# Reordering the start of a fused attention and MoE kernel: score bans ahead of their data, batch 2's scores ahead of batch 3's turn, MoE pieces moved in front of the first attention round

## The chip, the cores and the metric

The kernel runs on one core of a Trainium2 chip. The metric is device time in microseconds of one execution. Before the change it was 351.97 us, the median of three runs (351.76 to 352.08). PE is the matmul engine, DVE the vector engine, ACT the scalar engine, Pool the GpSimd engine; SP issues loads. A run is compared only with fast runs (executions that ran about as fast as the fastest of the same kernel).

## The reference

Eight batches of eight heads, 576 positions, head size 64. Forgetting attention (causal, with a decay from cumulated log gates), then a SiLU MoE layer with one expert over all 4608 tokens:

```python
scores = scale * q @ k.T + (cum[:, None] - cum[None, :])   # causal, log gates cumulated
attn   = softmax(scores); x = attn @ v                      # [4608, 512]
h = x @ w_in                                                # [4608, 2048]
out = (h * sigmoid(h)) @ w_out                              # [4608, 512], float32
```

## The kernel before

All engines' instruction orders are fixed by hand. The first 128 positions ("heads") of all batches are done first. For each batch: a *turn* (32 small matmuls, 16 for q and 16 for k, that transpose them, then copies out of PSUM by ACT and DVE), *scores* (8 matmuls, then an exp on ACT), *out* (8 matmuls with v, then a division on DVE), *back* (4 transposes of the result and a copy into x). Batches 0 to 3 form the first MoE group; when they are done the first MoE matmuls can start. Batches 4 to 7 are woven between MoE pieces, and then sixteen attention rounds for the other positions follow, R0 first, also woven with MoE pieces. A MoE piece is 4 matmuls: "m1" (x with w_in, tile `hp`) or "m2" (with w_out, tile `po`).

The causal mask is made in two ways. With a *ban*, two 128x512 matmuls put -30000 on the forbidden scores before the scores are added in PSUM, which costs PE time (0.53 us for two of them in the trace of before, 28.92 to 29.45 us). For batches 6 and 7 DVE multiplies the exponentials by a triangle after the exp instead (`mask0`).

```python
def ban0(b):                                   # needs no data of batch b
    sc = psc.tile([P, 2, NP, P], FP32, name="sc", tag="sc")      # psc: 2 buffers
    for i in range(2):
        nc.tensor.matmul(sc[:, i, :, :]..., lhsT=ident_bf, rhs=ban..., start=True, stop=False)
    return sc
# ... (cut)
def mask0(b):
    x = u0[b][:, :, :, :].rearrange("p i a t -> p (i a) t")
    nc.vector.tensor_tensor(out=x, in0=x, in1=tri[:, None, :].to_broadcast([P, H, P]), op=ALU.mult)
# ... (cut)
def convert_v(b, c):                           # weights v for an attention round, on Pool
    nc.gpsimd.tensor_tensor(out=vbf[b][r, c, :, :], in0=vst[b][c][r, :, :], in1=w_bf[...], op=ALU.mult)
# ... (cut)
keep_warm(1)                                   # one dummy 128x512 matmul
turn0(0, 1)
turn0(1, 0)
weights()
convert_v0(0); load_w_in(0)
scores0(0, ban0(0))
turn0(1, 1); turn0(2, 0); turn0(2, 1)
scores0(1, ban0(1))
convert_v0(1); load_v0(4)
out0(0, apart=True)
turn0(3, 0); turn0(3, 1)
scores0(2, ban0(2))
convert_v0(2); load_w_in(1); load_v0(5)
out0(1, apart=True)
back0(0, on_dve)
scores0(3, ban0(3))
convert_v0(3); load_qk0(4); load_w_in(2); load_qk0(5); load_w_in(3)
# ... (cut: out and back of batches 2 and 3, one more keep_warm(1))
load_qk(2); load_v(0, 2); load_v(0, 3); load_qk(3)      # loads for the rounds, on SP
for n in range(2):
    cast_qk(n); transposes(n)                            # Pool casts, SP transposes by DMA
# ... (cut: one more load)
for c in range(NM):
    convert_v(0, c)
fill(6.0)                                      # about 6 us of MoE pieces
two_more(4, True)                              # batches 4 and 5, banned
ready.add(1); fill(5.0); open2["w"] = True; fill(6.0, 2)
two_more(6, False)                             # batches 6 and 7, masked by DVE
```

The softmax here doesn't subtract the row's maximum and nothing guards it: scores larger than these inputs give would overflow.

## Time and profile before

| what | value |
|---|---|
| time | 351.97 us (351.76 to 352.08) |
| profiled execution | 351.23 us, span 349.5 us |
| PE busy | 340.0 us of 349.5 |
| first MoE matmul | 18.91 us |
| DMA share, every microsecond from 5 to 45 us | 1.16 or more (times of packets that overlap are added up, so it can pass 1) |

The head of the profile page: span and instruction count, then busy time of PE, and of part 2 (40 slices of the span, tenths) the granted PE clock and the DMA engines.

```profile
span 349.5 us, 9037 instructions
PE 340.0 (97%) x3645; PEld 204.3 (58%) x3645; DVE 188.8 (54%) x412; ACT 217.5 (62%) x400; POOL 123.6 (35%) x221
...
PEclk9999999999999999999999999999999999999999
DMA  8999999999996797596597589469620000010012
```

PE is busy nearly all the time (97%) at the full clock (mean 1.000), and DMA is full in the first eighth of the span (busy share 1.16 or more from 5 us on). So the only thing an order can win is PE's waits. The view of waits, for PE: engine, line, tile waited for, total us, times, longest (its first line, for the start-up dummies, is left out).

```profile
PE hp L544 <- ACT x L376: 0.8, 1, 0.8
PE tp L271 <- DMA qkb<-in_q_dram: 0.7, 1, 0.7
PE sc L445 <- ACT u L449: 0.5, 1, 0.5
PE tx L375 <- DVE xq L360: 0.5, 1, 0.5
PE dn L490 <- DVE gt L553: 0.4, 1, 0.4
PE dn L345 <- ACT u L312: 0.3, 1, 0.3
```

Where they stand, from PE's timeline: start, duration, operation, and in brackets the idle time before it and what ended it.

```profile
7.97 0.64 PE L271 MATMUL tp<-sel,qkb 128*64 128x64 bf16 x16 [0.75 <-DMA qkb<-in_q_dram]
18.91 1.46 PE L544 MATMUL hp<-x,w_in_bf 128*128 128x512 bf16 x6
38.83 5.40 PE L544 MATMUL hp<-x,w_in_bf 128*128 128x256 bf16 x48 [0.78 <-ACT x L376]
64.37 0.40 PE L445 MATMUL sc<-qkT 64*128 64x128 bf16 x8 [0.54 <-ACT u L449]
```

The first is batch 1's turn waiting for its q, the third the second MoE group waiting for ACT's copy, the last R0's scores waiting for an exp.

### The profile page before, as it was taken

Reading aid. Unit: us, or ns where it says so; the run is one execution under the profiler, and the core shown is the slowest. Engines: PE = TensorE matmul, PEld = TensorE weight load, DVE = VectorE, ACT = ScalarE, POOL = GpSimd, SP = SyncE. Lnnn points to the kernel's source line nnn. Section 1 sums busy time; section 2 is a strip of 40 time slices with the busy share of each in tenths; the row PEclk is TensorE's granted clock in tenths of the full one; section 3 lists DMA queues with packets and bytes.
Section 4 is the critical chain, followed back from the end, with each engine's and each line's share of the span. In section 5 each row is a group of like instructions: output and inputs, shape, how many; then the busy total and the mean of one; then the engine's idle time right before and its main releaser. Section 6 shows DMA issues by size and latency. Waiting matters only on the chain.

```text
span 349.5 us, 9037 instructions
## 1 busy us (share of the span) xinstructions
PE 340.0 (97%) x3645; PEld 204.3 (58%) x3645; DVE 188.8 (54%) x412; ACT 217.5 (62%) x400; POOL 123.6 (35%) x221
## 2 busy tenths in 40 slices
PE   7999999999999999999999999999999999999994
PEld 3645655566656656566565666656656565555663
DVE  4665925376666556466555664656745563534330
ACT  5766725886587675857768667595775934544431
POOL 7893156445282262273054225325320000010101
PEclk9999999999999999999999999999999999999999
DMA  8999999999996797596597589469620000010012
GB/s 159 226 205 201 198 199 196 240 184 189 196 205 152 155 148 172 124 199 152 125 206 145 125 189 147 114 160 188 130 54 34 32 32 30 30 63 30 32 60 60
DMA packets 136762, 47.92 MB, mean 137 GB/s; under 512 B 128017, under 2 KB 134417, under 8 KB 136721
## 3 DMA queue, kind: packets, MB, share of 16 engines
q1 hardware_dynamic: 127184, 31.75, 49.2%
q0 software_dynamic: 9376, 15.47, 18.7%
q8 instruction: 28, 0.46, 0.6%
q10 hardware_dynamic: 160, 0.13, 0.1%
q14 instruction: 14, 0.11, 0.1%
HBM read 36.85 MB, written 9.44 MB: 132 GB/s over the span
## 4 chain that ended last, share of the span: by engine, by line
PE 92%; ACT 3%; DMA 1%; issue 1%; DVE 1%; POOL 0%; POOLq 0%; ACTq 0%
PE po L589 36%; PE hp L544 35%; PE sc L445 7%; PE dn L490 5%; PE dn L499 3%; PE tp L271 2%; PE tx L520 2%; DMA qkb<-in_q_dram 1%; ACT u L449 1%; PE sc L286 1%; PE sc L305 1%; PE dn L345 1%; ACT osb L599 0%; PE tx L375 0%; ACT ut L461 0%
## 5 line engine op out<-in xcount | busy, mean ns | idle before, releaser
L552 ACT ACTIVATE th<-hp 128x384 bf16<-128x384 f32 (+2 forms) x208 | 95.4, 479 | 81.7 <-PE hp L544 79.9
L589 PE MATMUL po<-w_out_bf,gt 128*128 128x512 bf16 (+1 forms) x592 | 145.3, 374 | 0.0
L553 DVE SCALAR_TENSOR_TENSOR gt<-th,hp 128x384 bf16<-128x384 bf16 (+2 forms) x208 | 105.6, 522 | 70.6 <-ACT th L552 67.5
L544 PE MATMUL hp<-x,w_in_bf 128*128 128x384 bf16 (+2 forms) x704 | 128.8, 321 | 0.9 <-ACT x L376 0.8
L544 PEld LDWEIGHTS <-w_in_bf 128*128 128x128 bf16 x832 | 78.5, 98 | 53.9 <-issue 1.7
L449 ACT ACTIVATE u<-sc 128x1024 bf16<-128x1024 f32 (+1 forms) x96 | 74.9, 820 | 15.0 <-PE sc L445 15.0
L589 PEld LDWEIGHTS <-gt 128*128 128x128 bf16 x592 | 54.8, 98 | 49.8 <-issue 2.3
L568 POOL DMA_DIRECT2D out_dram<-osb x38 | 21.0, 553 | 174.0 <-ACT osb L599 138.5
L399 POOL TENSOR_TENSOR vp<-vf,w_bf 128x520 bf16<-128x520 f32 (+1 forms) x32 | 34.8, 1092 | 18.8 <-DMA vf<-in_v_dram 17.3
L454 DVE TENSOR_TENSOR u<-u,tri 128x768 bf16<-128x768 bf16 x32 | 23.1, 722 | 26.9 <-ACT u L449 26.9
L599 ACT ACTIVATE osb<-po 128x512 f32<-128x512 f32 (+1 forms) x37 | 22.0, 595 | 16.9 <-PE po L589 16.9
L445 PE MATMUL sc<-qkT 64*128 64x128 bf16 (+1 forms) x640 | 26.3, 207 | 0.5 <-ACT u L449 0.5
L445 PEld LDWEIGHTS <-qkT 64*128 64x128 bf16 x640 | 18.2, 94 | 9.9 <-issue 7.1
L461 ACT ACTIVATE ut<-sc 128x640 bf16<-128x640 f32 x32 | 23.1, 723 | 0.0
L468 DVE TENSOR_TENSOR ut<-ut,trit 128x128 bf16<-128x128 bf16 x32 | 7.8, 243 | 28.0 <-ACT ut L461 27.9
L490 PEld LDWEIGHTS <-u 128*128 128x128 bf16 x576 | 20.8, 97 | 3.4 <-issue 0.5
L490 PE MATMUL dn<-vp,u 128*128 128x65 bf16 x384 | 21.8, 193 | 0.0
L508 DVE TENSOR_TENSOR xr<-dn,rec 128x448 bf16<-128x448 f32 x32 | 20.0, 625 | 1.1
L490 PE MATMUL dn<-v,u 128*128 128x65 bf16 x192 | 19.8, 193 | 0.4 <-DVE gt L553 0.4
L385 POOL CAST qkb<-qf 128x384 bf16<-128x384 f32 x32 | 17.0, 532 | 4.1 <-DMA qf<-in_q_dram 3.6
L385 POOL CAST qkb<-kf 128x384 bf16<-128x384 f32 x32 | 17.2, 539 | 3.2 <-DMA kf<-in_k_dram 3.0
L544 PE MATMUL hp<-xt,w_in_bf 128*128 128x256 bf16 x128 | 17.7, 273 | 0.0
(67 smaller groups left out, 218.4 us busy)
## 6 DMA issues: line engine op xcount, KB each, us to landing
vf<-in_v_dram SPq DMA_DIRECT2D x32, 256.0 KB, 4.9
out_dram<-osb POOLq DMA_DIRECT2D x32, 256.0 KB, 2.7
qf<-in_q_dram SPq DMA_DIRECT2D x64, 96.0 KB, 3.0
kf<-in_k_dram SPq DMA_DIRECT2D x64, 96.0 KB, 3.0
w_in_bf<-in_moe_w_in_dram POOLq DMA_DIRECT2D x4, 512.0 KB, 8.7
w_out_bf<-in_moe_w_out_dram POOLq DMA_DIRECT2D x4, 512.0 KB, 12.9
qkb<-in_q_dram POOLq DMA_DIRECT2D x8, 128.0 KB, 6.0
qkb<-in_k_dram POOLq DMA_DIRECT2D x8, 128.0 KB, 6.2
```

Source lines behind the costliest of these rows:

```text
L385: nc.gpsimd.tensor_copy(out=t2[:, c0 : c0 + NR, :].rearrange("p c x -> p (c x)"), in_=t[:, :, :, :].rearrange("p c h d -> p (c h d)"),)
L399: nc.gpsimd.tensor_tensor(out=vbf[b][r, c, :, :], in0=vst[b][c][r, :, :], in1=w_bf[r, c + 1, b * H : (b + 1) * H, None].to_broadcast([n, H ...
L445: nc.tensor.matmul(sc[:, i, o : o + q1 - q0], lhsT=kt, rhs=t[r, q0:q1], start=True, stop=True)
L449: nc.scalar.activation(out=u[:, :, c * SM : c * SM + w], in_=sc[:, :, 0:w], func=ACT.Exp, scale=scale)
L454: nc.vector.tensor_tensor(out=x, in0=x, in1=tri[:, None, None, :].to_broadcast([P, 2, NR, P]), op=ALU.mult,)
L461: nc.scalar.activation(out=ut[:, :, 0:3:2, :].rearrange("p k i t -> p i k t"), in_=sc[:, :, T0 : T0 + (NM + 1) * ST].rearrange("p i (k t) ...
L490: nc.tensor.matmul(dn[:, i * NR + c - 1, :], lhsT=u[:, i, o : o + P], rhs=vals(kb, i), start=(kb == 0), stop=(kb == c),)
L544: nc.tensor.matmul(hp[:, :], lhsT=w_in_bf[:, cc, fc * P : (fc + 1) * P], rhs=xg(g)[:, cc, :], start=(cc == 0), stop=(cc == NCC - 1),)
L552: nc.scalar.activation(out=th[:, :], in_=hp[:, :], func=ACT.Tanh, scale=0.5)
L553: nc.vector.scalar_tensor_tensor(out=gt[:, fc, :], in0=th[:, :], scalar=1.0, in1=hp[:, :], op0=ALU.add, op1=ALU.mult,)
L589: nc.tensor.matmul(po[:, :], lhsT=gt[:, fc, tb * P : (tb + 1) * P], rhs=w_out_bf[:, fc, m0:m1], start=(fc == 0), stop=(fc == NFC - 1),)
L599: nc.scalar.activation(out=osb[:, :], in_=po[:, :], func=ACT.Copy, scale=0.5)
```

## The change

The intent: PE stands idle at 7.2 us waiting for batch 1, and the bans need no data, so the bans of batches 0 and 1 go into that hole. Batch 2's scores go ahead of batch 3's turn so that their exp runs earlier, one copy moves from DVE to ACT, one of the two single dummy matmuls goes, and MoE pieces are moved: one out of the first fill, some in front of R0.

```diff
@@ weights_scan @@
+        nc.vector.tensor_scalar(out=ban[:, :, :], in0=tri[...], scalar1=-1.0, scalar2=30000.0, ...)
@@ prologue @@
-    nc.vector.tensor_scalar(out=ban[:, :, :], ...)        # (cut: moved up)
     keep_warm(1)
     turn0(0, 1)
-    turn0(1, 0)
+    bans = [ban0(0), ban0(1)]
     weights()
 ...
-    scores0(0, ban0(0))
+    turn0(1, 0)
+    scores0(0, bans[0])
 ...
-    scores0(1, ban0(1))
+    scores0(1, bans[1])
 ...
     out0(0, apart=True)
-    turn0(3, 0)
-    turn0(3, 1)
     scores0(2, ban0(2))
     convert_v0(2)
     load_w_in(1)
     load_v0(5)
+    turn0(3, 0)
+    turn0(3, 1)
+    bans = ban0(3)
     out0(1, apart=True)
-    back0(0, on_dve)
-    scores0(3, ban0(3))
+    scores0(3, bans)
 ...
+    back0(0, on_act)
     out0(2)
     back0(1, on_act)
-    keep_warm(1)
     out0(3, 1)
 ...
-    fill(6.0)
+    fill(5.0)
     two_more(4, True)
 ...
     two_more(6, False)
     ready.add(2)
+    fill(2.5)
```

More of the change, by code (lines that the diff above doesn't have):

```diff
@@ L248, in weights_scan @@
             out=wexp[:, 0:S], in_=cum[:, :], func=ACT.Exp, bias=half[:, 0:1], scale=-1.0
+        )
+        nc.vector.tensor_scalar(
+            out=ban[:, :, :],
+            in0=tri[:, None, :].to_broadcast([P, NP, P]),
+            scalar1=-1.0,
+            scalar2=30000.0,
+            op0=ALU.add,
+            op1=ALU.mult,
         )
@@ L667 @@
     turn0(0, 0)
-    nc.vector.tensor_scalar(
-        out=ban[:, :, :],
-        in0=tri[:, None, :].to_broadcast([P, NP, P]),
-        scalar1=-1.0,
-        scalar2=30000.0,
-        op0=ALU.add,
-        op1=ALU.mult,
-    )
     keep_warm(1)
     turn0(0, 1)
-    turn0(1, 0)
+    bans = [ban0(0), ban0(1)]
     weights()
```

## The prediction

> **What bounds it now.** PE. The page shows PE busy 340.0 of 349.5 us, clock at full, and the chain of waits is 92% PE. PE's idle time, read from its timeline: 1.20 at the start, about 2.7 up to 39 us, 0.54 (63.8, scores waiting for ACT exp), 0.37 (79.5), 0.24 (113), about 4.5 of tail after the last matmul. Reordering can win some 3.8 us, 1%.
>
> **What the change moves.** One dummy 128x512 matmul (about 0.22 us at its neighbours' spacing) goes; the rest only moves.
>
> 1. *Bans first.* PE idles 7.23-7.97 waiting for batch 1's q. Four ban matmuls (about 0.9 us) move into that gap. The weight transposes then come at about 7.95 instead of 8.54, batch 0's scores at about 8.96 instead of 9.53, batch 1's at 10.75 instead of 11.86.
> 2. *Batch 2's scores before batch 3's turn, two ACT copies instead of DVE.* Batch 3's exp, which ended at 16.91 and held up its attention (0.32), ends near 15.7. Four more steps (2.0 us before) lead to the first MoE matmul: ready near 17.7 instead of 18.91.
> 3. *But the loads do not come earlier.* DMA share is 1.2 or more in every microsecond from 5 to 45 us, about 205 GB/s. The first w_in quarter lands at 18.1, the second at 21.7, batch 5's q at 26.5 and k at 27.15 (issue plus time to landing). Batch 2's v lands at 12.5 and holds Pool, so the issues behind it move by about 0.1. [...] So I expect new PE waits: about 0.3 at the second w_in quarter and about 1.2 before batch 5's turn, because `fill(5.0)` also brings that turn one MoE piece (0.87) earlier. The lead of step 2 is spent there: about 0.4 us behind the old kernel near 28 us, equal work counted.
> 4. *The piece saved is spent where PE waited.* It now stands after batch 5's transposes, where PE idled 0.78 (38.05-38.83) for ACT's copy. That gap goes. Second-stage start near 38.5 instead of 38.83: net gain of the prologue 0.3-0.4 us.
> 5. *`fill(2.5)` and rebalance.* The same work before R0, interleaved from about 41 us instead of 44 (w_out's last quarter lands at 42.85, needed about 44: enough). In R0's first slot two more pieces (0.43 + 0.87) stand between the scores, so the 0.54 us wait at 63.8 goes. The waits at 79.5 and 113 stay: that order is unchanged. Tail unchanged.
>
> Sum: -0.35 (prologue, dummy matmul included) -0.54 (R0) = about -0.9 us.
>
> **Predicted:** 351.0 us, range 350.2 to 351.9. Chances: faster by over 2% 0.01, within 2% 0.98, slower by over 2% 0.01.
>
> **What would show it.** Right: PE gap at 7.2 gone; first MoE matmul at 17.6-18.2; PE waiting about 1 us for DMA of batch 5's q near 25-26.5; no gap at 38; no exp wait in R0; PE busy total down about 0.2.
> Wrong: batch 5's q landing well before 26 us (then up to 1 us more gain, near 350).
>
> **What would make it wrong.** Another interleaving of the two load queues shifting landings by a microsecond; new waits for PSUM buffers where pieces follow each other faster than ACT and DVE drain them; the second of two attention rounds waiting for other pieces; the transposed q and k of R0 not ready when R0 starts.

## More of the kernel before

One more thing to keep for later is DVE's mask of batch 6, and the Pool weighting that starts just after it (DVE's and Pool's timelines):

```profile
56.22 0.69 DVE L321 TENSOR_TENSOR u<-u,tri 128x1024 bf16<-128x1024 bf16 x1 [2.21 <-ACT u L312]
...
56.33 1.49 POOL L399 TENSOR_TENSOR vp<-vf,w_bf 128x520 bf16<-128x520 f32 x1 [2.47 <-DMA vf<-in_v_dram]
```

## The result

The changed kernel took 351.59 us (351.40 to 351.81, 4 runs) beside 351.87 us for the kernel before (351.36 to 352.08). The ratio is 0.9994, 95% interval 0.9977 to 1.0012. A ratio is the mean time of one kernel's fast runs over that of the other's of the same rounds, so it is not quite the ratio of the medians. A repeat with more rounds, reported below, gave 0.9981 (0.9967 to 0.9994). So the repeat shows a gain of 0.2 to 1.2 us, the first rounds alone show none that is clear of noise, and both exclude 2%.

The profile after, head of the page (its busy time of PE is not comparable with the one before, because 47 matmul records are missing from this trace: 3597 against 3644 weight loads):

```profile
span 349.9 us, 8986 instructions
PE 337.1 (96%) x3597; PEld 204.5 (58%) x3644; DVE 187.1 (53%) x411; ACT 217.5 (62%) x401; POOL 123.1 (35%) x221
...
DMA  8999989899798797597496598479611000010012
```

PE's waits after the change (the first two lines, for the start-up dummies and for gaps without a releaser, are left out):

```profile
PE tp L279 <- DMA qkb<-in_q_dram: 0.8, 1, 0.8
PE dn L353 <- DVE u L329: 0.8, 1, 0.8
PE hp L552 <- DMA w_in_bf<-in_moe_w_in_dram: 0.6, 1, 0.6
PE hp L552 <- DVE gt L561: 0.3, 1, 0.3
PE tx L383 <- DVE xq L368: 0.3, 1, 0.3
PE dn L498 <- DVE gt L561: 0.3, 1, 0.3
```

And where they stand on PE's timeline:

```profile
7.25 1.04 PE L294 MATMUL sc<-ban,ident_bf 128*128 128x512 bf16 x4
18.27 5.55 PE L552 MATMUL hp<-x,w_in_bf 128*128 128x512 bf16 x23 [0.58 <-DMA w_in_bf<-in_moe_w_in_dram]
26.58 1.29 PE L279 MATMUL tp<-sel,qkb 128*64 128x64 bf16 x32 [0.78 <-DMA qkb<-in_q_dram]
37.84 3.90 PE L552 MATMUL hp<-x,w_in_bf 128*128 128x512 bf16 x28
55.58 0.43 PE L353 MATMUL dn<-v,u 128*128 128x65 bf16 x8 [0.77 <-DVE u L329]
```

The hole at 7.2 us is filled by the four bans. PE was free for the first MoE matmul at 17.68 but got its weights at 18.27. Batch 5's turn waits 0.78 us for its q. The waits at 38 us and at R0's exp are gone. A wait that was not there before stands at 55.6 us: batch 6's attention waits for DVE's mask.

DVE's mask of batch 6 and the Pool weighting beside it, after:

```profile
54.02 1.51 DVE L329 TENSOR_TENSOR u<-u,tri 128x1024 bf16<-128x1024 bf16 x1 [0.50 <-ACT u L320]
...
53.92 1.05 POOL L407 TENSOR_TENSOR vp<-vf,w_bf 128x520 bf16<-128x520 f32 x1 [0.18 <-DMA vf<-in_v_dram]
```

The same instruction takes 1.51 us instead of 0.69. This time Pool started 0.1 us before it.

**A ledger of lost time.** The orders differ, so start times cannot be subtracted directly. I took each of PE's weight loads in program order and subtracted from its start time the nominal time of all matmuls before it. Nominal times are the median distances in these traces: 0.216 us for a 512-wide matmul, 0.163 for 384, 0.109 for 256, 0.052 for 128, 0.029 for 65, and 0.031 for the turns' small ones, an estimate (in the trace of before 48 of them take 1.46 us, from 9.86 to 11.32, and 32 take 1.01, from 25.05 to 26.06). What remains is time lost up to that point, plus a constant that is the same for all columns. Only differences between columns of one row mean something. The kernel before has one dummy matmul (0.22 us) more of work on top. Values in us; the experiments are told below.

| up to | before | after | after, repeat | front alone | Pool held | SP order |
|---|---|---|---|---|---|---|
| second MoE piece | 8.43 | 8.01 | 8.07 | 7.60 | 7.62 | 7.82 |
| end of batch 5's turn | 9.44 | 10.27 | 9.89 | 9.39 | 9.67 | 9.89 |
| second m2 piece | 10.74 | 11.07 | 10.69 | 10.70 | 10.48 | 10.70 |
| batch 6's back | 12.05 | 13.13 | 12.50 | 12.00 | 12.01 | 12.23 |
| R0's attention | 12.54 | 13.02 | 13.00 | 12.50 | 12.74 | 12.22 |
| last m2 matmul | 9.86 | 10.45 | 10.45 | 10.35 | 10.79 | 9.66 |

After the change PE is 0.42 us ahead at the second MoE piece (0.64 with the dummy), 0.83 behind at the end of batch 5's turn, 0.33 behind at the m2 pieces, 1.08 behind after batch 6, and 0.48 behind in R0.

In these two profiled executions the changed kernel thus ends 0.37 us *later*, and the timed runs say the opposite. The execution of the kernel before that was profiled took 351.23 us. Over all rounds the kernel before ran 48 times with a mean of 352.06 us, from 351.07 to 353.77, and only one of the 48 was below 351.23. The changed kernel's profiled 351.62 lies in the middle of its ten runs (mean 351.51, 350.95 to 352.03). So the trace of before shows nearly its best case. What the slower executions of the kernel before lose could not be seen, as none was profiled. The waits below are therefore shown, but where the timed gain comes from is not.

### The profile page after: what moved, and what is told of

Same layout as the page of the kernel before. It is cut to its first block, busy times and chain, and to the rows that moved or that the text cites. A ratio compares the mean times of both kernels' runs of the same rounds, so it can differ in the third digit from the quotient of the medians.

```text
span 349.9 us, 8986 instructions
## 1 busy us (share of the span) xinstructions
PE 337.1 (96%) x3597; PEld 204.5 (58%) x3644; DVE 187.1 (53%) x411; ACT 217.5 (62%) x401; POOL 123.1 (35%) x221
## 3 DMA queue, kind: packets, MB, share of 16 engines
HBM read 36.85 MB, written 9.44 MB: 132 GB/s over the span
## 4 chain that ended last, share of the span: by engine, by line
PE 88%; DMA 4%; ACT 3%; issue 2%; DVE 1%; POOL 0%; ACTq 0%; POOLq 0%
PE po L597 35%; PE hp L552 32%; PE sc L453 7%; PE dn L498 5%; PE dn L507 3%; DMA qkb<-in_q_dram 3%; PE tp L279 2%; PE tx L528 2%; DMA qkb<-in_k_dram 1%; ACT u L457 1%; PE sc L294 1%; PE sc L313 1%; PE dn L353 1%; DVE gt L561 1%; ACT ut L469 0%
## 5 line engine op out<-in xcount | busy, mean ns | idle before, releaser
L597 PE MATMUL po<-w_out_bf,gt 128*128 128x512 bf16 (+1 forms) x550 | 139.9, 373 | 2.9 <-issue 1.1
L462 DVE TENSOR_TENSOR u<-u,tri 128x768 bf16<-128x768 bf16 x32 | 20.8, 651 | 23.9 <-ACT u L457 23.9
L476 DVE TENSOR_TENSOR ut<-ut,trit 128x128 bf16<-128x128 bf16 x32 | 9.0, 281 | 28.1 <-ACT ut L469 28.0
L498 PE MATMUL dn<-vp,u 128*128 128x65 bf16 x384 | 21.8, 193 | 0.0
L393 POOL CAST qkb<-qf 128x384 bf16<-128x384 f32 x32 | 16.2, 508 | 10.5 <-DMA qf<-in_q_dram 7.8
L552 PE MATMUL hp<-xt,w_in_bf 128*128 128x256 bf16 x128 | 17.7, 273 | 0.1
```

Source lines behind the costliest of these rows:

```text
L393: nc.gpsimd.tensor_copy(out=t2[:, c0 : c0 + NR, :].rearrange("p c x -> p (c x)"), in_=t[:, :, :, :].rearrange("p c h d -> p (c h d)"),)
L498: nc.tensor.matmul(dn[:, i * NR + c - 1, :], lhsT=u[:, i, o : o + P], rhs=vals(kb, i), start=(kb == 0), stop=(kb == c),)
L552: nc.tensor.matmul(hp[:, :], lhsT=w_in_bf[:, cc, fc * P : (fc + 1) * P], rhs=xg(g)[:, cc, :], start=(cc == 0), stop=(cc == NCC - 1),)
L597: nc.tensor.matmul(po[:, :], lhsT=gt[:, fc, tb * P : (tb + 1) * P], rhs=w_out_bf[:, fc, m0:m1], start=(fc == 0), stop=(fc == NFC - 1),)
```

## The experiments

All gave correct results. Five timed rounds each, in four groups, each group on another chip with the kernel before beside it. In the table, the waits of PE up to R0 are those of the profiled execution that the argument turns on. Left out are waits of up to 0.61 us for the first loads before 7 us (0.59 in e_front, 0.61 in e_buf4, 0.46 in e_pool) and of 0.30 to 0.53 us for DVE near 17 us, which every run has.

| run | median, us | ratio to before (95%) | waits of PE up to R0, us |
|---|---|---|---|
| e_front | 351.59 | 1.0000 (0.9971 to 1.0028) | second w_in quarter 0.61, ACT's copy 0.78, R0's exp 0.54 |
| e_fills | 351.74 | 0.9994 (0.9973 to 1.0015) | batch 1's q 0.44, batch 5's q 0.70, mask 0.21 |
| e_qk5 | 351.76 | 0.9991 (0.9967 to 1.0016) | first w_in quarter 0.88, mask 0.80 |
| e_pool | 351.67 | 0.9989 (0.9963 to 1.0014) | w_in 0.25, batch 5's q 0.35, transposed q and k of R0 0.66 |
| e_v45 | 353.84 | 1.0054 (1.0037 to 1.0071) | v of batch 4 0.30, w_out 1.22, mask 0.84, transposed q and k 0.45 |
| e_buf4 | 351.34 | 0.9984 (0.9965 to 1.0004) | w_in 0.65 and 0.22, batch 5's q 0.47, transposed q and k 0.19 |
| e_sp | 351.50 | 0.9984 (0.9965 to 1.0003) | w_in 0.40, batch 5's q 0.25 |
| e_all | 354.92 | 1.0079 (1.0058 to 1.0101) | w_out 0.36 and 1.19, v of batch 5 0.59; later 1.68 |
| e_again | 351.43 | 0.9981 (0.9967 to 0.9994) | w_in 0.36, mask 0.17, transposed q and k 0.44 |
| e_best1 | 352.22 | 1.0004 (0.9988 to 1.0021) | w_in 1.15; later 0.98 |
| e_best2 | 356.05 | 1.0110 (1.0090 to 1.0130) | v of batch 5 3.58 |
| e_warm | 351.69 | 0.9997 (0.9977 to 1.0017) | w_in 0.73, batch 5's q 0.82 |

Theory A: the new front does start the MoE earlier, and the loads, which fill the DMA from 5 to 45 us, take it back. Theory C: the new wait at batch 6 comes from DVE and Pool meeting. The rivals are that the fills carry the gain, that another limit (PSUM, ACT) holds PE at the same places, and that the waits are bare accidents of single executions.

### The front alone

```diff
-    fill(5.0)
+    fill(6.0)
     two_more(4, True)
 ...
-    fill(2.5)
```

> The changed kernel with the fills put back as they were (6.0 before batch 4's turn, none after batch 7). Theory A (the new order of the prologue does start the MoE about 0.6 us earlier, and the loads take most of it back): first MoE matmul at 18.2-18.4 us, PE wait for batch 5's q shrinks from 0.78 to about 0.0-0.2 because one more MoE piece (0.87 us) stands before it, the 0.78 us wait for ACT's copy near 38 us comes back, second-stage start about 38.3; no 0.77 us wait of batch 6's attention for the mask; the 0.54 us wait for exp in the first attention round comes back. Time about 0.4 us below the kernel before. Rival B (the fills carry what gain there is): same time as the kernel before, within 0.2.

The first MoE matmul came at 17.87 us, a full 1.04 us earlier than in the kernel before and earlier than expected. The first w_in quarter landed at 17.1 here. Four pieces later PE stood still for the second quarter, and the two old waits were back:

```profile
PE hp L552 <- ACT x L384: 0.8, 1, 0.8
PE hp L552 <- DMA w_in_bf<-in_moe_w_in_dram: 0.6, 1, 0.6
PE sc L453 <- ACT u L457: 0.5, 1, 0.5
```

In the ledger it is 0.83 us ahead of the kernel before at the second MoE piece and level with it (0.05) at the end of batch 5's turn. From there on it only keeps the 0.22 us of the dummy matmul that it lacks, and it loses 0.5 more in a later wait at 80 us (0.91 instead of 0.37 for `gt`). Theory A holds for the mechanism. The expected 0.4 us is not shown: the timed ratio is not able to tell either way. Five of its six runs have a mean of 351.50, the sixth took 353.84 with a mean clock of 0.992 (see e_warm); setting it apart is a choice made afterwards, and the kernel before had such a run (353.77, clock 0.993) in the same rounds.

### The fills alone

The kernel before, with `fill(5.0)` for `fill(6.0)` and `fill(2.5)` after batch 7.

> The kernel before with the two new fills alone (5.0, and 2.5 after batch 7). Theory A: first MoE matmul at 18.9; PE waits 0.3-0.6 us for batch 5's q; the wait for ACT's copy near 38 us goes (-0.78); the exp wait in the first attention round goes (-0.54); a wait of batch 6's attention for the mask of 0.3-0.8 us comes. Time within 0.4 us of the kernel before. Rival B: 0.3-0.8 us faster than the kernel before.

Batch 5's q was waited for 0.70 us, ACT's copy and R0's exp were not waited for, and the mask was (0.21). Its median is 0.04 us from that of before. So the fills trade waits: 0.78 and 0.54 go, 0.70 and 0.21 come, and more is lost between (in the ledger R0's attention stands at 12.91 against 12.54). The rival, that they carry a gain of 0.3 us or more, is not supported, but the interval (down to 0.9973, or 0.95 us) does not exclude it.

### Batch 5's q and k issued earlier

```diff
     load_qk0(4)
-    load_w_in(2)
     load_qk0(5)
+    load_w_in(2)
```

> The changed kernel with batch 5's q and k issued ahead of the third w_in quarter. Theory A (DMA is full and serves its queue in order, so what is issued first lands first): batch 5's q and k land 1.5-2.5 us earlier, the 0.78 us PE wait before batch 5's turn goes, the third w_in quarter lands later but before it is read near 29 us; everything after is 0.7-0.8 us earlier, time about 0.7 us below the changed kernel. Rival: something else (PSUM buffers, ACT) holds PE at that place and the wait only changes its name; time equal to the changed kernel.

Batch 5's q landed at 24.3 and its k at 25.0 us instead of 26.5 and 27.2, as theory A expects. In the traces of before and after, Pool's loads of the first 30 us land in the order of their issue throughout (before: the third w_in quarter issued at 16.55 and landed at 25.82, batch 5's q 17.34 and 26.53, its k 17.85 and 27.16, the fourth quarter 18.36 and 29.67). The wait before its turn was gone too, but this run does not show that the landing was the reason: PE came to the turn only at 27.42, when the loads in their old order would have been there as well. Cleaner are e_all and e_best2, told below, which came to it at 25.02 and 25.29 without a wait. The third w_in quarter landed at 27.5 instead of 25.9, and nothing waited for it. PE was late in this execution for another reason. PE's wait for the first w_in quarter was 0.88 us, and then the granted clock fell to half. The stretches view (PE, PEld, DVE, ACT, Pool busy; granted clock; DMA share; GB/s):

```profile
15.40:18.80 3.40, 2.01 (x19) 1.08 (x21) 2.04 (x6) 2.25 (x5) 3.40 (x6) 1.00 1.25 225
18.80:22.20 3.40, 3.29 (x9) 1.22 (x8) 0.69 (x1) 1.03 (x2) 3.13 (x11) 0.51 1.24 203
22.20:25.60 3.40, 3.40 (x21) 1.44 (x21) 2.35 (x4) 2.02 (x5) 3.38 (x4) 0.99 1.24 204
```

From the first MoE weight load to batch 4's turn the six pieces took 6.98 us here and 5.48 us in the changed kernel: 1.5 us lost to the clock (512-wide matmuls with a median of 634 ns between 17.3 and 20 us, 379 in the changed kernel). Read in stretches of a microsecond, the granted clock was 0.92 from 18 to 19 us, 0.50 from 19 to 22 and 0.87 from 22 to 23, which makes about 3.4 us at half. Before that PE was busy for 2.01 of 3.40 us (15.40 to 18.80). What made the clock fall is not shown: in e_warm PE was busy for 2.02 us of the same stretch, and its clock was 0.999 over the execution, where this one has 0.994.

### Pool held back until the mask is done

```diff
-    for c in range(NM):
-        convert_v(0, c)
 ...
                 scores0(b + x)
                 mask0(b + x)
+                if x == 1:
+                    nc.gpsimd.tensor_copy(out=junk2[0:1, :], in_=u0[b + x][0:1, 0, 0, 0:16])
+                    for c in range(NM):
+                        convert_v(0, c)
```

> The changed kernel with Pool's four weightings of v for the first attention round held back until DVE has masked batch 7 (a 16-element Pool copy that reads the masked tile stands ahead of them). Theory C (DVE's mask of batch 6 took 1.51 us instead of 0.69 [...]): mask of batch 6 at 0.69 us, the 0.77 us PE wait of batch 6's attention goes, time 0.6-0.8 us below the changed kernel. Rival D (too few MoE pieces between batch 7's scores and batch 6's attention, Pool has no part): mask still longer than 1.2 us or the wait stays above 0.4 us, time equal to the changed kernel.

Theory C is that the mask is slow because Pool's weighting runs beside it.

```profile
53.42 0.69 DVE L330 TENSOR_TENSOR u<-u,tri 128x1024 bf16<-128x1024 bf16 x1 [0.49 <-ACT u L321]
...
PE sc L454 <- DMA qkT<-qkb: 1.2, 2, 0.7
```

The mask took 0.69 us, and the wait of batch 6's attention fell from 0.77 to nothing of note. Theory C holds for the mask and D falls; the expected 0.6 to 0.8 us of time did not come (the median is 0.08 above the changed kernel's first rounds). In four profiles with Pool held back (e_pool, e_sp, e_best1, e_best2) the mask took 0.69 us. In four where Pool's weighting started first, it took 1.51 us (after), 0.91 (e_again), 1.27 (e_buf4) and 0.94 (e_fills), and it ended 0.54 to 0.56 us after that weighting (after: 55.53 and 54.97; e_again 54.54 and 53.99; e_buf4 54.40 and 53.86; e_fills 55.49 and 54.94), whatever its start. That is 0.13 to 0.15 us less than the 0.69 us it takes otherwise (the profile calls its spans on Pool rough). In the kernel before, where the mask was first, it was Pool's that was longer, 1.49 instead of 1.05 us. How the two get in each other's way is not shown.

The second line of the fence says why the time did not follow. R0 now stood ready at 60.9 us, and the transposed q and k that it needs were not there until 61.56.

### Batch 4's and 5's v later

```diff
     convert_v0(1)
-    load_v0(4)
 ...
     load_w_in(1)
+    after(w_in_bf[...])        # SP goes on when the second w_in quarter has landed
+    load_v0(4)
     load_v0(5)
```

> The changed kernel with the loads of v for batches 4 and 5 (256 KB each, not read before 31 us) sent only after the second w_in quarter has landed. Theory A (the prologue is bound by the order of bytes on a full DMA): first w_in quarter lands about 1 us earlier (17.0-17.5), first MoE matmul at 17.5-17.8 without a DMA wait, no wait at the second quarter, batch 5's q lands 0.5-1.5 us earlier and the 0.78 us wait shrinks below 0.3; PE at the first 256-wide MoE matmul 0.8-1.3 us earlier than in the changed kernel (38.5). Rival: the landings are set by something other than bytes ahead in the queue (latency, Pool's issue times) and stay within 0.3 us; then nothing moves.

The first w_in quarter landed at 16.7 (18.2 in the changed kernel), the second at 19.5 (21.8), and PE waited for neither. The end of batch 5's turn stands at 9.35 in the ledger, 0.92 better than the changed kernel. That confirms that what stands ahead in the queues sets these landings (whether its bytes or the number of its packets, the run does not tell). It is no accident of one execution: in e_v45 and e_all, which hold these loads back, the first quarter landed at 16.7 (issued at 10.7 and 10.4), and in the nine with the changed kernel's order of loads, listed below, at 17.1 or later. The 512 KB were then owed later: v of batch 4, issued at 20.1, took until 29.9 to land, 9.8 us (in the kernel before, issued at 10.81, it took 4.9; batch 5's v, issued at 12.68, took 10.4). Pool stood still for it until 29.98, sent w_out from 30.98 instead of 23.14, and PE paid at its second-group m2 pieces:

```profile
PE po L597 <- DMA w_out_bf<-in_moe_w_out_dram: 1.2, 1, 1.2
```

The run is 1.9 us slower than the kernel before.

### Four buffers for the transposed q

`qktp` with `bufs=4` instead of 3.

> The changed kernel with four buffers instead of three for the transposed q (and k). ACT's copies of batch 5's and 7's q no longer wait for the scores of batch 4 and 6, so exp and mask of batch 6 start about 0.5 us earlier. Theory C (the mask lost 0.8 us to Pool's weighting because it started 0.1 us after it): mask of batch 6 starts before Pool's second weighting, takes 0.69 us, and the 0.77 us PE wait of batch 6's attention goes; then R0 waits for the transposed q and k (0.3-0.7 us) because they land no earlier. Time within 0.4 us of the changed kernel. Rival D: mask time unchanged at 1.5 us, wait only 0.5 us shorter by the earlier start.

The wait of batch 6's attention went, but not as theory C said. The mask still met Pool's weighting (1.27 us), only a microsecond earlier, when there was time for it. So neither expectation fits whole: the mask stayed slow, as rival D says, but the wait went altogether. R0 waited 0.19 us for transposed q and k.

### First transposes earlier on SP

On top of the Pool-held kernel:

```diff
-    load_qk(2); load_v(0, 2); load_v(0, 3); load_qk(3)
     for n in range(2):
         cast_qk(n); transposes(n)
+    load_qk(2); load_v(0, 2); load_v(0, 3); load_qk(3)
```

> The Pool-held kernel of before (mask wait gone, new waits of 0.66 and 0.56 us for transposed q and k) with the two first transposing loads sent ahead of the loads of rounds 2 and 3 on the SP queue. Theory E (the first attention round cannot start before SP's queue has come to its transposes): they go out 3-5 us earlier (about 51-53), the 0.66 us wait at R0 goes, R0 starts near 61; what is delayed behind them (q, k of rounds 2 and 3) costs nothing or moves the 0.56 us wait of round 2. Time 0.3-0.9 us below the Pool-held kernel. Rival: DMA bandwidth sets the landing, and R0 still waits over 0.4 us.

SP's queue, first the changed kernel, then this one:

```profile
56.58 2.83 SPq L421 DMA_TRANSPOSE qkT<-qkb  x2
```

```profile
50.09 2.79 SPq L422 DMA_TRANSPOSE qkT<-qkb  x2
```

They went out 6.5 us earlier and R0 waited for nothing. The ledger has it at 12.22 in R0's attention, 0.80 better than the changed kernel, and it keeps that to the end (9.66 against 10.45). Theory E holds. It also explains a riddle of the ledger. The changed kernel's profile and its repeat lost 13.13 and 12.50 us up to batch 6, yet both stand at 13.0 in R0: what the repeat had won before R0 it waited off there (0.44 us). In the first profile the transposed q and k landed at 61.45 and R0 started at 61.85, so at most 0.40 us of its 0.77 us mask wait could have been won. The fills brought this limit: in the kernel before and in e_front these loads landed at 59.2 and 59.3, with `fill(2.5)` at 61.4 to 61.8 (after, e_again, e_fills, e_pool, e_buf4). Why they took longer then was not followed up. The timed ratio of 0.9984 is no better than the changed kernel's own 0.9981, though. One of the six runs has a clock of 0.994; the mean of the other five is 351.32 us, but the ratio keeps all six.

### All repairs at once, and two attempts at a better version

e_all joins e_v45, e_qk5, e_buf4 and the SP order. e_best1 is e_sp with e_qk5 and e_buf4. e_best2 adds v of batches 4 and 5 behind the *first* w_in quarter, with w_out issued ahead of their weighting.

> The changed kernel with all the repairs that leave the arithmetic alone: v of batches 4 and 5 later, batch 5's q and k ahead of the third w_in quarter, four buffers for transposed q, first transposes earlier on SP. Theory (the change's gain was taken back by loads, the mask wait and the start of R0): the waits of 0.57, 0.78 and 0.77 us go and nothing of their size replaces them; R0's first attention 1.5-2 us earlier than in the changed kernel; time 1.3-2.0 us below the changed kernel, about 350.0. Rival: another limit (PSUM buffers, or Pool and DVE in the attention rounds) takes at least half of it back; time above 350.9.

> The changed kernel with batch 5's q and k ahead of the third w_in quarter, four buffers for transposed q, Pool's weightings behind the mask, and the first transposes early on SP. Theory: no wait for batch 5's q, none for the mask, none at R0; what is left in the prologue is 0.3-0.9 us for w_in. 0.8-1.3 us below the changed kernel, and at least 1.0 us below the kernel before. Rival (a new wait of like size each time one is removed): within 0.4 us of the changed kernel.

> As the run before it, and v of batches 4 and 5 sent after the first w_in quarter has landed, with Pool issuing w_out ahead of its weightings of that v (the earlier attempt lost 1.2 us at w_out because Pool stood still for v until 30 us). Theory: no waits for w_in and w_out; v of batch 4 lands by 27 us, early enough; 1.3-2.0 us below the changed kernel. Rival: the bytes are owed somewhere; a wait of 0.5 us or more comes at batch 4's or 5's attention, at w_out or at batch 6's turn, and the time is that of the run before it or above.

All three miss. e_all had the best start of any run (8.50 at the end of batch 5's turn, 1.77 better than the changed kernel), then paid 0.59 for v, 1.55 for w_out and 1.68 for round 1's transposed q and k. e_best1 had its first w_in quarter late (1.15 us), fell to half the clock as e_qk5 did (PE busy for 1.79 of the 3.40 us from 15.40 to 18.80, granted clock 0.56 in the next 3.40), and lost 0.98 us to transposed q and k in round 1. In e_best2 v of batch 5 came to Pool only at 35.26, PE stood still for 3.58 us, and the clock fell to half in that execution; all its six runs have a mean clock of 0.988 to 0.993:

```profile
33.50:36.90 3.40, 0.54 (x10) 0.42 (x10) 1.04 (x3) 0.00 (x0) 1.64 (x3) 1.00 1.22 196
36.90:40.30 3.40, 3.40 (x14) 1.51 (x13) 1.54 (x4) 1.26 (x3) 1.52 (x3) 0.55 1.23 199
```

The rivals of these three were right in substance: each time other waits of like size came. In e_all and e_best2 they were for the loads that had been put back. In e_best1 nothing had been put ahead of the first w_in quarter, which was late by scatter. Why four buffers together with the early transposes make round 1 wait (e_all and e_best1 do; e_sp, with three, does not; nor does e_best2, where PE was later by then) was not followed up and stays open.

### The changed kernel again

> The changed kernel itself, unaltered, for a tighter interval beside the next two. Theory A+C (front gain taken back by loads, mask and R0): 0.0 to 0.4 us below the kernel before; waits of 0.3-0.8 us at w_in or batch 5's q (which of the two is a matter of the execution) and 0.7-0.8 us before batch 6's attention in its profile. Rival (the recorded prediction's sum was right and the first measurement was unlucky): 0.8-1.0 us below the kernel before.

The ratio is 0.9981, about 0.67 us (352.1 times 0.0019). Its interval excludes no gain at all. It also excludes neither 0.3 nor the forecast 0.9. The waits are of the expected kinds but not of the expected places: 0.36 at the second w_in quarter, the mask 0.17 instead of 0.77, and R0 0.44. At batch 5's turn there was none.

### Dummy matmuls put back

The SP-order kernel with `keep_warm(2)` ahead of `out0(3, 1)`, where the change had dropped one.

> The kernel with Pool's weightings behind the mask and the first transposes early on SP, and two dummy 128x512 matmuls put back where the change had dropped one (before batch 3's attention). Theory F (after the change PE is busy for only 1.8-2.2 of the 3.4 us before the first MoE matmul, and where the first w_in quarter comes late the granted clock falls to half for 3.41 us, which costs 1.4 us in about one execution of seven): the dummies lie in time that PE waits anyway, so the first MoE matmul is at most 0.2 us later; no execution of the six shows a clock below 0.996; median within 0.3 us of the same kernel without dummies, at least 0.7 us below the kernel before. Rival: the dummies cost their 0.43 us in full, or a clock below 0.996 still comes.

No run had a clock below 0.996, and the first MoE matmul waited 0.73 us for w_in, which landed at 18.7 this time, so the dummies cost nothing there. But the median was 351.69 us, ratio 0.9997, and the expected 0.7 us below the kernel before did not come. Half of the expectation failed. Whether the dummies keep the clock up is not shown: without them a clock below 0.996 came in 1 of 6 runs of each of e_front, e_qk5, e_buf4, e_sp and e_best1, in 2 of 6 of e_all, in all 6 of e_best2, in none of 10 runs of the changed kernel and in none of 6 of e_pool and of e_v45. The kernel before, which has the dummy, had it in 1 of the 44 runs whose clock is known. The 1.4 us and the one in seven of theory F are estimates: the clock cost 1.5 us in e_qk5, and the runs named here without e_best2 had a clock below 0.996 in 7 of 58 executions.

**How much single executions differ.** Nine profiled executions have the same order of loads up to the first w_in quarter (the changed kernel, its repeat, e_front, e_qk5, e_pool, e_buf4, e_sp, e_best1, e_warm). The quarter was issued at 10.3 to 10.9 us in all of them and landed anywhere from 17.1 to 18.8. That is more than the change's whole gain. It is why one profile must not be read to the tenth of a microsecond here.

No version was shown to beat both kernels. e_sp and e_buf4 have the lowest ratios beside the changed kernel's repeat, and their intervals overlap with it and with 1.

## Why the prediction was right or wrong

The forecast of 351.0 us with a range of 350.2 to 351.9 and "within 2%" held: 351.59. Neither says much. The range holds the kernel before itself (351.87 beside it), and nobody expected 2%. The steps are the test. The measured gain was 0.2 us by the ratio of the first rounds and 0.67 by the repeat, against a forecast of about 0.9. The first series' interval (down to 0.9977) excludes the forecast ratio (351.0/351.97 = 0.9972), the second's does not. Step by step:

1. *Bans first.* Right. The hole at 7.23 to 7.97 is gone. Batch 0's scores came at 9.24 and batch 1's at 11.03 (forecast 8.96 and 10.75), in part because the four bans took 0.97 us in place of about 0.9, and batch 0's k landed 0.10 later than in the other trace.
2. *First MoE matmul ready near 17.7.* Right: PE was free at 17.68, and in e_front and e_pool, where w_in was there in time, it started at 17.87 and 17.89. (The step speaks of two copies given to ACT; the change moves one.)
3. *The loads do not come earlier, and take the lead back.* Right in mechanism, and it was the step that mattered most. Forecast 0.3 at the second w_in quarter and 1.2 before batch 5's turn, together 1.5. Measured 0.58 at the first quarter and 0.78 before the turn, together 1.36, in the repeat 0.36 at the second and none at the turn, in e_front 0.61 at the second and none at the turn. That the sum came close in one execution is in part luck, since the landings scatter by 1.7 us. e_qk5 and e_v45 confirm by the landings that it is the order of loads on a full DMA (batch 5's q at 24.3 instead of 26.5; the first w_in quarter at 16.7 instead of 18.2). The DMA moved 209 GB/s from 5 to 45 us after the change; why not more was not tested.
4. *The piece saved goes where PE waited 0.78 us.* Right: no wait at 38 us. The net gain of the prologue was forecast at 0.3 to 0.4 us. The second group's matmuls started at 38.70 (37.84 plus four times 0.216) against 38.83: 0.13. In the ledger, with the dummy counted, the two executions stand 0.11 behind and 0.27 ahead of the kernel before at the second m2 piece.
5. *R0's exp wait of 0.54 goes.* Right for the wait itself, and wrong in the sum. It was counted as a gain of 0.54. What the runs showed in its place is that the same rearrangement makes batch 6's mask meet Pool's weighting (0.77 us in one execution, 0.17 in the other), and that R0 cannot start before SP's transposes (0.44 in the repeat, where the mask wait was small). Either way R0's attention stands at 13.0 in the ledger. This is the term of the sum that was mis-sized: in place of minus 0.54, the ledger has plus 0.15 and plus 0.51 in the two executions between the second m2 piece and R0's attention. The late transposes were named in the list of what could go wrong. The meeting of DVE and Pool was not; the list has new waits for PSUM buffers only.
6. *PE's busy total down by 0.2.* Not testable with 47 records missing.

Not foreseen at all: that the clock can fall after waits before the first MoE matmul, seen in two of the variants' profiles (mean granted clock from 18.80 to 22.20 us 0.51 in e_qk5, after a wait of 0.88 us, and 0.56 in e_best1, after 1.15). No limit comes out of these traces: e_warm, with a wait of 0.73 there, kept 0.999 over its execution, and e_all, with a later wait of 1.68, kept 0.998.

## What to carry to other kernels

When loads fill the DMA from the start, moving compute earlier can move the wait from compute to a load (here 0.58 us for w_in and 0.78 us for batch 5's q), so list the landing times first and read off how early each consumer may be; a load moved ahead pushes others back (1.6 us for the third w_in quarter in e_qk5, without cost; w_out in e_v45, at 1.22 us of wait), so look at when those are read. A list-scheduled engine that is 97% busy hides several limits of equal height, and removing a half-microsecond wait can show the next one (here the mask against Pool, 0.77 us, then SP's queue, 0.44 us), so check every producer of the next common meeting point, here R0, before counting a gain. For effects near 0.2%, profile more than one execution of each kernel: the same load landed over a range of 1.7 us.
